# One core, linear attention and a gated FFN: half units in pairs, 12 gated units, one more q transposed by TensorE, single stores, another order

## The chip, the core and the metric

The kernel runs on one core of a Trainium2 chip. The metric is the device time of one execution in microseconds. The five engines each take their own instructions in order: TensorE (PE, with its weight loads PEld), VectorE (DVE), ScalarE (ACT), GpSimd (POOL) and SyncE (SP), which here issues nearly all DMAs. An engine's part that issues and waits is written with a q (SPq, ACTq).

## The reference

```python
def _attn_ref(q, k, v):                      # 8 batches, 8 heads, 576 tokens, 64 wide
    q_s = np.exp(q - np.max(q, axis=-1, keepdims=True))
    q_s = q_s / (np.sum(q_s, axis=-1, keepdims=True) + 1e-09)
    k_s = np.exp(k - np.max(k, axis=2, keepdims=True))      # over the tokens
    k_s = k_s / (np.sum(k_s, axis=2, keepdims=True) + 1e-09)
    kv = np.einsum('bhsd,bhse->bhde', k_s, v)
    return np.einsum('bhsd,bhde->bhse', q_s, kv)

def _moe_ref(x, w_in, w_out, beta):          # x: 4608 x 512, w_in 512 x 2048, w_out 2048 x 512
    h = x @ w_in
    g = h * (1.0 / (1.0 + np.exp(-beta * h)))
    return g @ w_out
```

x is the attention's output with the heads side by side. All inputs and the output are float32.

## The kernel before

**Layout.** A batch's 576 tokens are read as 64 x 9: token p*9 + i lies on partition p, with two heads' 64 partitions on top of each other, so that four tiles j hold eight heads. i = 0 to 7 are the main part (512 tokens), i = 8 the tail (64 tokens). There are nine chunks of 512 tokens: one per batch, and one (number 7, `TAILS`) with the tails of all eight; the chunk behind it, number 8, is batch 7.

**Attention of a batch b.** VectorE takes the maxima of q (`q_max`, L360) and POOL subtracts them (`q_sub`, L376); ScalarE takes the exponential (`q_exp`, L383); VectorE sums and inverts (`q_sum` L406, `q_rcp` L412 and L413); POOL scales and casts to bf16 (`q_norm`, L421). Then q must be transposed. Batch 0 does that on TensorE (`q_tr`, L442, with evictions by `q_tr_ev`); batches 1 to 7 do it with a DMA that SyncE issues (`q_tr_dma`, L428). For k, VectorE takes maxima over the tokens (`k_max` L462, `k_red` L473, `k_small` L494 and L497, `k_rep` L515), POOL subtracts (`k_sub`, L525), ScalarE takes the exponential (`k_exp`, L532). `kv_mm` (L556) makes kv in two PSUM banks, 72 small matmuls; `kv_norm` (L575 to L578, VectorE) makes kvn from it; `x_mm` (L606) multiplies kvn with the transposed q into four banks, and `x_ev` casts each of them into xT, the FFN's input, with tokens in the order (i, p). `xt_mm` (L645) and `xt_ev` do the tail.

**FFN.** A unit n is one chunk and one block of 128 of the 2048 inner columns, so there are 9 x 16 = 144 units. `st1` (L758) makes h in one PSUM bank with 4 matmuls of 512 columns; `tanh` (L774, ScalarE) and `gate` (L787, VectorE, out = (tanh + 1) * h) make g, in one of NG = 8 buffers; `st2` (L825, and L817 for the last quarter of the last chunk) adds g's product into four banks `acc`, one per 128 tokens, with 4 matmuls. At the end of a chunk `o_ev` copies the banks into osb, and `store` (L854) issues two DMAs for each 128 tokens, as each half holds the rows of another i. The first four units (`LEAD`) go in halves of 256 tokens: a bank holds one unit, and each half has a tanh and a gate of its own.

**Banks.** Four PSUM banks (`ring`) go round among h, kv, x and tails (`take`): the next taker gets the bank that was taken longest ago and is free by then.

**The order** is written out by hand: `ORDER` names every step once (h_5 is the first stage of unit 5, th_5 and g_5 its tanh and gate, o_5 its second stage, ld_ a load, st_ a store, qT_ a DMA transpose), with the engine behind = where it can be chosen. Each engine gets its instructions in this order; the semaphores between engines follow from the data. So a load or store that must wait holds up all that stands behind it on SyncE, and a maximum whose load is late holds up the gates behind it on VectorE. In the built program each DMA also waits for the landing of the one eight before it. Before the first FFN matmul TensorE runs dummy matmuls (`fill`, L349). The weights come in eight loads of two halves; each half is cast to bf16 on POOL or ScalarE.

Of the kernel before, what the change touches and what calls it, by code (L numbers as in the profile page):

```python
# [17 lines left out]
ld_q0_0, consts, qmax_0_2_0, qmax_0_0_0, qsub_0_0_0=pool, qmax_0_1_0, qexp_0_0_0, qsub_0_2_0=pool, ld_q0_1,  # L18
qmax_0_0_j3, qmax_0_2_1, ld_k0_1, qmax_0_1_1, qmax_0_0_j2, qexp_0_0_j3, qsum_0_0_0, ld_beta, kmax_0_1, ld_k0_0,
qsub_0_1_1=pool, qsub_0_1_0=pool, kmax_0_0, qsub_0_2_1=pool, fill_0, fill_1, fill_12, fill_13, beta_tr, fill_8,  # L20
fill_10, qexp_0_0_j2, fill_2, fill_9, qexp_0_1_0, qrcp_0_0, kred_0, fill_11, qexp_0_1_1, qexp_0_2_0, ld_v0_1,
vcast_0_j3=pool, kswap_0, ld_v0_0, qsum_0_1_0, qsum_0_2_0, qnorm_0_0_0=pool, qtr_0_0_0, ksmall_0, qsum_0_1_1,
krep_0_0, krep_0_1, ksub_0_2=dve, ksub_0_0=dve, qnorm_0_0_1=pool, vcast_0_j0=act, qexp_0_2_1, qsum_0_2_1,
vcast_0_j1=act, ksub_0_3=pool, vcast_0_j2=pool, fill_15, ld_q1_1, qrcp_0_1, fill_4, fill_14, qtrev_0_0_0=act,
kexp_0_2, qtr_0_0_1, kexp_0_3, kexp_0_0, ld_w0_1, ld_w0_0, ld_k1_1, ksub_0_1=dve, kexp_0_1, fill_16, kv_0_1, beta_ev,
kv_0_0, qmax_1_3, cast_w0_0_1=act, qmax_1_2, ld_w1_0, ld_w2_0, qnorm_0_1_0=pool, qnorm_0_1_1=pool, qtr_0_1_0,
qtr_0_1_1, fill_3, kvn_0, cast_w0_1_1=act, qtrev_0_1_0=act, qtrev_0_0_1=dve, x_0_0_1, x_0_0_0, xev_0_0_0=act,
cast_w0_1_0=pool, fill_5, qrcp_0_2, qtrev_0_1_1=dve, cast_w0_0_0=pool, xev_0_0_1=dve, qsub_1_1=pool, fill_7, x_0_1_1,
x_0_1_0, h_0_0_0, h_0_0_1, h_2_0_0, xev_0_1_0=act, qnorm_0_2_1=pool, kmax_1_3, xev_0_1_1=dve, th_0_0, g_0_0, h_3_0_0,
fill_6, cast_w2_0=pool, h_3_0_1, qexp_1_3, qnorm_0_2_0=pool, th_3_0, ld_w2_1, qexp_1_2, h_1_0_0, h_1_0_1, h_0_1_0,  # L30
h_2_0_1, cast_w1_0=pool, cast_w2_1=pool, ld_w1_1, h_2_1_0, h_2_1_1, h_0_1_1, h_3_1_0, th_1_0, h_1_1_0, ld_k1_0,
h_1_1_1, h_3_1_1, ld_w4_1, qsum_1_3, ld_w4_0, kmax_1_2, th_0_1, qsum_1_2, g_0_1, ld_w3_0, th_2_0, th_1_1, th_2_1,
ld_q1_0, ld_w3_1, o_0_0, th_3_1, g_3_0, g_2_0, g_2_1, qrcp_1_1, o_0_1, h_5, cast_w1_1=pool, qnorm_1_1=pool, ld_w6_1,
cast_w4_1=pool, g_3_1, g_1_0, g_1_1, kmax_1_1, kmax_1_0, kred_1, th_5, ksmall_1, h_4, g_5, o_1_0, th_4, h_6, th_6,
krep_1, g_4, o_1_1, h_7, o_2_0, o_2_1, o_3_0, cast_w4_0=pool, g_6, cast_w3_0=act, h_8, th_7, th_8, ld_w5_0, qmax_1_0,
qmax_1_1, ld_w6_0, ksub_1_0=pool, o_3_1, h_9, th_9, qsub_1_0=pool, h_11, o_4, cast_w3_1=act, o_5, o_6, g_7, o_7, g_8,
ld_w5_1, ld_q2_1, h_10, cast_w5_0=pool, cast_w6_1=act, th_11, ld_v1_1, qexp_1_1, ld_w7_0, o_8, g_11, qexp_1_0, g_9,
qsum_1_0, qsum_1_1, ksub_1_1=pool, cast_w6_0=act, th_10, qtrt_0, qtrtev_0_0=act, h_12, cast_w5_1=act, kexp_1_3, o_9,
h_14, kexp_1_0, th_12, qtrtev_0_1=dve, qrcp_1_0, kexp_1_1, th_14, g_10, qmax_2_2, qmax_2_3, qnorm_1_0=pool, h_15,
h_13, ld_v1_0, ld_w7_1, cast_w7_0=act, g_14, g_12, th_13, g_13, vcast_1_1=pool, qsub_2_1=pool, kexp_1_2, th_15, g_15,  # L40
vcast_1_0=pool, o_10, o_11, qexp_2_3, qexp_2_2, o_12, o_13, cast_w7_1=pool, qsum_2_3, kv_1_0, kv_1_1, o_14, qT_1,
kvn_1, qsum_2_2, x_1_1, x_1_0, xev_1_2=act, xev_1_0=dve, xev_1_3=dve, xev_1_1=act, qrcp_2_1, ld_q2_0, o_15, h_17_0,
qmax_2_0, ld_v2_1, ld_k2_1, ld_k2_0, h_17_1, qmax_2_1, oev_0_3=act, th_17, ld_q3_0, h_16_0, g_17, h_16_1, th_16,
g_16, ld_v2_0, ld_k3_0, h_18, th_18, oev_0_2=act, g_18, kmax_2_3, h_24, oev_0_0=act, h_21, th_21, kmax_2_0,
qnorm_2_1=pool, kmax_2_1, h_20, oev_0_1=act, qsub_2_0=pool, g_21, h_19, o_16, o_17, h_22, th_20, kmax_2_2, o_18,
qmax_3_0, g_20, th_19, g_19, ld_v3_0, qexp_2_1, th_24, th_22, kred_2, ksmall_2, vcast_2_1=pool, h_23, g_22, krep_2,
ld_k3_1, th_23, qmax_3_1, g_23, qexp_2_0, kmax_3_2, ld_q3_1, h_26, st_0_1, o_19, o_20, h_25, vcast_2_0=act, g_24,
qsum_2_1, kmax_3_3, ld_q4_0, o_21, h_27, qsum_2_0, th_26, o_22, vcast_3_0=pool, ksub_2_1=pool, kexp_2_2, th_25, g_26,
g_25, kexp_2_3, ksub_2_0=pool, th_27, o_23, g_27, ld_v3_1, o_24, o_25, xt_0, kexp_2_0, kexp_2_1, kv_2_0, kv_2_1,
xtev_0_0=act, xtev_0_1=act, h_30, h_28, kmax_3_0, qrcp_2_0, qnorm_2_0=pool, kmax_3_1, qsub_3_0=pool, qmax_3_2, kvn_2,  # L50
qmax_3_3, kred_3, th_30, th_28, g_28, st_0_3, qsub_3_1=pool, vcast_3_1=pool, h_29, o_26, ld_q4_1, h_31, st_0_0,
ld_k4_1, st_0_2, th_29, ksmall_3, g_29, g_30, qT_2, th_31, o_27, o_28, o_29, g_31, krep_3, x_2_1, xev_2_3=act, x_2_0,
xev_2_0=dve, xev_2_2=dve, qexp_3_1, ld_k4_0, o_30, o_31, xev_2_1=act, kmax_4_1, qexp_3_2, h_34, oev_1_2=act, th_34,
ksub_3_0=pool, ksub_3_1=pool, h_32, oev_1_1=dve, th_32, oev_1_3=act, qmax_4_1, h_33, oev_1_0=act, th_33, qexp_3_3,
g_34, g_32, ld_v4_1, h_35, qsum_3_1, ld_v4_0, th_35, st_1_1, ld_q5_1, h_37, h_36, qmax_4_3, kexp_3_3, g_33, th_36,
qmax_4_2, th_37, g_35, qmax_4_0, o_32, g_37, qsum_3_2, g_36, vcast_4_1=pool, vcast_4_0=pool, h_38, kexp_3_0, o_33,
th_38, h_39, qsum_3_3, qsub_4_1=pool, qexp_3_0, kexp_3_1, qsub_4_0=pool, th_39, g_39, qrcp_3_1, h_42, o_34, qsum_3_0,
kexp_3_2, th_42, g_38, h_40, th_40, g_40, qnorm_3_1=pool, o_35, ld_k5_1, o_36, o_37, st_1_2, ld_q5_0, g_42, xt_1,
xtev_1_0=act, qrcp_3_0, xtev_1_1=dve, kmax_4_0, kmax_4_2, kv_3_0, kv_3_1, xt_2, kvn_3, xtev_2_1=dve, qmax_5_2,
kmax_4_3, kred_4, ksmall_4, xtev_2_0=act, o_38, o_39, o_40, h_43, qnorm_3_0=pool, h_41, qT_3, qexp_4_2, qexp_4_3,  # L60
th_43, g_43, th_41, g_41, kmax_5_2, krep_4, h_46, ld_k5_0, qexp_4_0, th_46, qexp_4_1, h_44, h_45, th_45, th_44, g_46,
o_41, o_42, st_1_3, o_43, g_44, x_3_0, st_1_0, g_45, x_3_1, ksub_4_1=pool, qsum_4_3, qmax_5_3, ksub_4_0=pool, o_44,
xev_3_2=act, h_47, th_47, xev_3_0=act, kmax_5_0, o_45, xev_3_1=dve, o_46, qsum_4_2, qsum_4_0, kmax_5_3, xev_3_3=act,
h_48, th_48, h_50, qsum_4_1, g_47, h_51, qsub_5_1=pool, h_49, g_48, th_50, qmax_5_0, g_50, ld_v6_1, th_51, h_52,
o_47, th_49, g_49, oev_2_1=dve, h_53, h_54, qrcp_4_1, g_51, oev_2_2=act, th_52, g_52, qnorm_4_1=pool, h_57, kmax_5_1,
kexp_4_2, oev_2_0=act, oev_2_3=dve, h_56, st_2_3, qexp_5_3, th_54, qexp_5_2, qrcp_4_0, o_48, o_49, ld_q7_1, st_2_0,
g_54, kred_5, qsum_5_3, o_50, qnorm_4_0=pool, th_53, qmax_5_1, o_51, h_60, qsub_5_0=pool, g_53, th_57, g_57, h_55,
th_56, g_56, th_55, o_52, th_60, g_60, h_59, ksmall_5, kexp_4_0, th_59, krep_5, g_59, ld_v5_1, h_62, ld_v5_0, qT_4,
qexp_5_0, kexp_4_3, st_2_1, st_2_2, o_53, h_63, th_63, th_62, kexp_4_1, o_54, h_58, ld_q6_1, g_55, g_62, o_55,
qsum_5_0, ksub_5_1=pool, kexp_5_3, th_58, o_56, o_57, g_58, qsum_5_2, qexp_5_1, g_63, ksub_5_0=pool, o_58, h_61,  # L70
kv_4_0, kv_4_1, ld_q7_0, ld_q6_0, qmax_6_3, qmax_6_2, kexp_5_2, th_61, kvn_4, o_59, g_61, o_60, qsum_5_1, qrcp_5_1,
qrcp_5_0, x_4_1, x_4_0, xev_4_1=dve, o_61, xev_4_0=act, o_62, kexp_5_1, o_63, xev_4_3=dve, oev_3_1=dve,
qsub_6_1=pool, xev_4_2=act, h_64, th_64, g_64, h_66, th_66, h_65, g_66, ld_k6_1, ld_v6_0, h_69, h_67, oev_3_0=dve,
th_65, g_65, th_69, qmax_6_0, g_69, h_68, oev_3_2=act, th_67, h_72, th_68, oev_3_3=act, qnorm_5_0=pool,
qnorm_5_1=pool, vcast_6_1=pool, g_68, g_67, vcast_5_1=pool, kmax_6_3, ld_v7_1, th_72, kexp_5_0, kmax_6_2, ld_k7_1,
st_3_3, ld_k6_0, qmax_7_3, h_75, ld_k7_0, o_64, h_70, th_70, h_71, g_70, th_71, o_65, qmax_7_2, o_66, o_67, g_72,
# [39 lines left out]
def kernel(  # L116
# [29 lines left out]

# [779 lines left out]
```

## Time and profile before

| | us |
|---|---|
| median of 3 runs (lowest, highest) | 293.31 (292.52, 293.66) |
| the profiled execution | 294.5 |
| its span, from first to last instruction | 292.7 |
| PE, DVE, ACT, POOL busy | 276.3, 199.6, 170.4, 130.7 |
| DMA queue of SyncE and ScalarE (q1), share of 16 engines | 57.3% |
| 140 tanhs of 512 columns, mean | 0.687 |
| 140 gates of 512 columns, mean | 0.680 |
| casts of xT, ScalarE and VectorE, mean | 0.587, 0.678 |
| 70 half stores of 128 KB, issue to landing, median | 2.4 |

The page gives busy times and 40 slices of the span with tenths of busy time; times in a timeline count from the span's start. "[3.84 <-DMA qf...]" behind a line is the idle time of the engine before it, and what ended it. PEclk is the clock granted to TensorE, in tenths of full speed.

### The profile page before, as it was taken

How to read it: one execution, taken by the hardware profiler on the slowest of the kernel's cores; microseconds unless marked ns; L12 is line 12 of the kernel's file. 1: busy time of each engine (PE TensorE's matmuls, PEld its weight loads, DVE VectorE, ACT ScalarE, POOL GpSimd, SP SyncE). 2: the span in 40 equal slices, each digit the busy share in tenths (PEclk: the TensorE clock that was granted, in tenths of full speed). 3: DMA queues.
4: the chain of work that ended last, by engine and by line, in shares of the span. 5: the costliest groups of instructions: out<-in, count | busy, mean ns of one | idle time of the engine just before them, and what ended most of it. 6: DMA issues, size and time to landing. Idle time of an engine off the chain costs nothing.

```text
span 292.7 us, 5174 instructions
## 1 busy us (share of the span) xinstructions
PE 276.3 (94%) x1922; PEld 128.7 (44%) x1951; DVE 199.6 (68%) x414; ACT 170.4 (58%) x297; POOL 130.7 (45%) x92
## 2 busy tenths in 40 slices
PE   7589999999999999996999999999999999999993
PEld 2255444444444544443344444444444444445551
DVE  3898867899799989774598968654754362456250
ACT  3687797866596656681375456845754255245342
POOL 5698986737987292661816473742002000000000
PEclk9889999999999999999799999999999999999999
DMA  7999999999954860699466908200410450005006
GB/s 247 392 391 385 386 380 208 394 383 357 231 185 155 209 215 0 176 229 304 164 204 226 179 23 164 61 2 0 111 34 2 81 125 21 0 1 129 17 0 143
DMA packets 39736, 50.60 MB, mean 173 GB/s; under 512 B 18576, under 2 KB 18848, under 8 KB 39712
## 3 DMA queue, kind: packets, MB, share of 16 engines
q1 hardware_dynamic: 39552, 50.15, 57.3%
q8 instruction: 15, 0.25, 0.3%
q10 hardware_dynamic: 160, 0.13, 0.2%
q14 instruction: 9, 0.07, 0.1%
HBM read 36.71 MB, written 9.44 MB: 158 GB/s over the span
## 4 chain that ended last, share of the span: by engine, by line
PE 73%; DMA 9%; DVE 6%; ACT 4%; issue 2%; SPq 2%; POOL 1%; POOLq 1%; ACTq 0%; DVEq 0%
PE hT L758 36%; PE acc L825 33%; DMA kf<-in_k_dram 6%; ACT th L774 2%; DMA qT<-qn 2%; DVE g L787 2%; DMA qf<-in_q_dram 1%; PE hT L606 1%; PE hT L556 1%; SPq L854 1%; ACT ek L532 1%; POOL kf L525 1%; DVE qs L406 1%; DMA out_dram<-osb 1%; POOLq L921 1%
## 5 line engine op out<-in xcount | busy, mean ns | idle before, releaser
L774 ACT ACTIVATE th<-hT,beta_c 128x512 bf16<-128x512 f32 (+1 forms) x148 | 97.1, 675 | 73.8 <-PE hT L758 59.4
L787 DVE SCALAR_TENSOR_TENSOR g<-th,hT 128x512 bf16<-128x512 bf16 (+1 forms) x148 | 94.8, 665 | 59.0 <-ACT th L774 56.7
L825 PE MATMUL acc<-w_out_b,g 128*128 128x512 bf16 x543 | 132.6, 381 | 1.3 <-issue 0.8
L758 PE MATMUL hT<-xT,w_in_b 128*128 128x512 bf16 (+1 forms) x519 | 119.1, 372 | 1.2 <-DVE g L787 0.7
L758 PEld LDWEIGHTS <-w_in_b 128*128 128x128 bf16 x592 | 57.6, 98 | 66.5 <-issue 1.2
L825 PEld LDWEIGHTS <-g 128*128 128x128 bf16 x560 | 53.8, 98 | 65.1 <-issue 4.3
L421 POOL TENSOR_TENSOR qn<-eq,qz 128x1152 bf16<-128x1152 bf16 (+2 forms) x20 | 34.6, 1738 | 50.8 <-DVE qz L413 35.0
L525 POOL TENSOR_TENSOR kf<-kf,kmb 128x1152 f32<-128x1152 f32 (+1 forms) x15 | 37.9, 2544 | 15.8 <-DVE kmb L515 10.0
L376 POOL TENSOR_TENSOR qf<-qf,qm 128x1152 f32<-128x1152 f32 (+2 forms) x19 | 33.3, 1768 | 20.1 <-DVE qm L360 13.2
L360 DVE TENSOR_REDUCE qm<-qf 128x9 f32<-128x576 f32 (+3 forms) x35 | 23.2, 688 | 8.3 <-DMA qf<-in_q_dram 8.2
L462 DVE TRANSPOSE_TENSOR_REDUCE km<-kf 128x18 f32<-128x576 f32 (+1 forms) x30 | 23.7, 803 | 1.8 <-DMA kf<-in_k_dram 1.6
L383 ACT ACTIVATE eq<-qf 128x576 bf16<-128x576 f32 (+2 forms) x33 | 20.9, 653 | 5.2 <-POOL qf L376 4.2
L406 DVE TENSOR_REDUCE qs<-eq 128x9 f32<-128x576 bf16 (+2 forms) x33 | 23.1, 706 | 0.1
L532 ACT ACTIVATE ek<-kf 128x576 bf16<-128x576 f32 x32 | 21.3, 684 | 2.4 <-POOL kf L525 2.3
L226 ACT CAST xT<-hT 128x512 bf16<-128x512 f32 x15 | 8.3, 587 | 18.7 <-PE hT L606 18.7
L228 POOL CAST va<-vf 128x1152 bf16<-128x1152 f32 (+1 forms) x14 | 14.9, 1080 | 7.7 <-DMA vf<-in_v_dram 7.7
L226 ACT COPY osb<-acc 128x512 f32<-128x512 f32 x23 | 13.0, 585 | 4.8 <-PE acc L825 2.2
L758 PE MATMUL hT<-xTt,w_in_b 128*128 128x512 bf16 x62 | 14.7, 379 | 0.1
L228 DVE COPY osb<-acc 128x512 f32<-128x512 f32 (+1 forms) x13 | 8.3, 659 | 7.0 <-PE acc L825 6.1
L349 PE MATMUL hT<-g,warm 128*128 128x512 bf16 x25 | 9.7, 512 | 1.6 <-POOL g L234 1.5
L228 DVE CAST xT<-hT 128x512 bf16<-128x512 f32 x13 | 8.3, 678 | 3.1 <-PE hT L606 3.0
L606 PE MATMUL hT<-qT,kvn 64*64 64x512 bf16 x56 | 5.4, 418 | 2.9 <-DVE kvn L578 2.5
(62 smaller groups left out, 106.5 us busy)
## 6 DMA issues: line engine op xcount, KB each, us to landing
qf<-in_q_dram SPq DMA_DIRECT2D x16, 576.0 KB, 5.0
kf<-in_k_dram SPq DMA_DIRECT2D x16, 576.0 KB, 7.3
vf<-in_v_dram SPq DMA_DIRECT2D x16, 576.0 KB, 7.6
out_dram<-osb SPq DMA_DIRECT2D x70, 128.0 KB, 2.4
wst<-in_moe_w_in_dram SPq DMA_DIRECT2D x8, 512.0 KB, 11.3
wst<-in_moe_w_out_dram SPq DMA_DIRECT2D x8, 512.0 KB, 11.1
out_dram<-osb SPq DMA_DIRECT2D x2, 64.0 KB, 2.0
out_dram<-osb ACTq DMA_DIRECT2D x2, 64.0 KB, 2.4
```

What stands on the lines that cost most here:

```text
L228: eng.tensor_copy(dst, src)
L360: dve.tensor_reduce(qm[:, j : j + n, i0:i1], qf[b % 2][:, j : j + n, i0:i1], axis=AX.X, op=ALU.max, negate=negate,)
L376: eng.tensor_tensor(x, x, m, ALU.subtract)
L406: dve.tensor_reduce(qs[:, i0:i1, j : j + n, 0:1], eq[:, i0:i1, j : j + n, :], axis=AX.X, op=ALU.add)
L421: eng.tensor_tensor(qn[b % 2][:, i0:i1, j : j + n, :], eq[:, i0:i1, j : j + n, :], z, ALU.mult)
L462: dve.tensor_reduce(km[:, j : j + n].rearrange("p j i e -> p (j i e)"), kf[b % 2][:, j : j + n].rearrange("p j i (e c) -> p (j i e) c", c=32),
L525: eng.tensor_tensor(x, x, m, ALU.subtract)
L532: act.activation(ek[b % 2][:, j : j + n], kf[b % 2][:, j : j + n], ACTF.Exp)
L758: pe.matmul(place[("h", n)][:, cols(h)], w_in_b[:, kt, u * P : (u + 1) * P], x[:, kt, cols(h)], start=(kt == 0), stop=(kt == KT - 1),)
L774: act.activation(th[n % 3][:, cols(h)], place[("h", n)][:, cols(h)], ACTF.Tanh, scale=beta_c[:, u : u + 1])
L787: dve.scalar_tensor_tensor(out=g[n % NG][:, cols(h)], in0=th[n % 3][:, cols(h)], scalar=1.0, in1=place[("h", n)][:, cols(h)], op0=ALU.add, ...
L825: pe.matmul(acc[t][:], g[n % NG][:, t * P : (t + 1) * P], w_out_b[:, u, :], start=(u == 0), stop=(u == NJ - 1),)
```

## The change

- **Half units in pairs.** For the first four units a bank now holds the same 256 tokens of two units (0 and 1, or 2 and 3). Each has its tanh; one gate does both, four gates of 512 columns for eight of 256.
- **12 gated units.** NG = 12; the buffers lie in pairs, so that one gate can write two.
- **Batch 1's q** is transposed by TensorE, 16 transposes and 2 for the tail, with four evictions, in place of the DMA. Batches 2 to 7 keep the DMA.
- **One store per 128 rows.** xT and xTt now hold tokens in an order in which a block of 128 alternates between two values of i; the evictions of x write every second element. A block's rows then lie in pairs next to each other in the output, and one DMA does them. The last quarter goes in two halves of 256 columns, one from SyncE, one from ScalarE.
- **A new order** of all steps, with other engines for some casts and evictions. Each engine's instructions stand in a new sequence.
- A path that would subtract k's maxima on TensorE is there, and not in use (`KPE` is empty); a constant for it, `minus`, is still made on POOL.

```diff
-    NG = 8
+    KPE = range(0)
+    NG = 12
...
-    g = [sbt(f"g{i}", [P, 512], BF16) for i in range(NG)]
+    gq = [sbt(f"g{i}", [P, 2, 512], BF16) for i in range(NG // 2)]
+    g = [gq[i // 2][:, i % 2] for i in range(NG)]
...
+        pool.memset(minus[:], 0.0)
+        pool.affine_select(
+            out=minus[:],
...
+    def mixed(x):
+        return x.rearrange("p (t c i) -> p t i c", i=2, c=64)
...
-        cast(eng, xT[b % 2][:, j, :], place[("x", b, j)])
+        cast(eng, mixed(xT[b % 2][:, j, :]), place[("x", b, j)].rearrange("p (t i c) -> p t i c", i=2, c=64))
...
-        op(f"qT {b}", lambda b=b: q_tr_dma(b))
+        if b > 1:
+            op(f"qT {b}", lambda b=b: q_tr_dma(b))
+            continue
+        for J in range(2):
+            op(f"qtr {b} {J}", lambda b=b, J=J: q_tr(b, J, 0, NM))
+            op(f"qtrev {b} {J}", lambda e, b=b, J=J: q_tr_ev(b, J, 0, NM, e), "act")
+            op(f"qtrtev {b} {J}", lambda e, b=b, J=J: q_tr_ev(b, J, NM, 1, e), "act")
+        op(f"qtrt {b}", lambda b=b: [q_tr(b, J, NM, 1) for J in range(2)])
...
+    def bank(n, h):
+        key = ("h", n) if h is None else ("hp", n // 2, h)
+        if key not in place:
+            take(key)
+        if h is None:
+            return place[key]
+        return place[key][:, 256 * (n % 2) : 256 * (n % 2) + 256]
...
+            out = gq[n // 2][:, :, cols(h)]
+            of = th[turn(n, h) % 3][:].rearrange("p (m t) -> p m t", m=2)
+            src = place[("hp", n // 2, h)].rearrange("p (m t) -> p m t", m=2)
+        dve.scalar_tensor_tensor(out=out, in0=of, scalar=1.0, in1=src, op0=ALU.add, op1=ALU.mult)
...
-    def store(c, t, engs=(sp, sp), x=None):
+    def store(c, t, eng=sp, x=None):
...
+            rows = out[b * S : (b + 1) * S, :].rearrange("(p i) f -> p i f", i=NI)[:, 2 * t : 2 * t + 2]
+        eng.dma_start(rows[:, :, f], osb[:, t, f])
```

The places in the new order that the prediction speaks of:

```python
..., kv_2_0, kv_2_1, xt_0, xtev_0_0=act, ld_k4_0, o_21, xtev_0_1=dve, qnorm_2_0=pool, qsub_3_0=pool, o_22, ...
o_23, o_24, kvn_2, o_25, o_26, qsub_3_1=pool, g_31, qexp_3_2, kmax_3_2, g_30, kred_3, qsum_3_2, qT_2, x_2_0, ...
st_1_3, ksub_4_0=pool, qT_3, st_1_2, ..., g_46, ld_q6_1, qmax_6_2, ld_k5_1, kmax_5_2, ld_q6_0, ...
st_2_3, ..., ld_q7_1, ld_v6_0, vcast_6_0=act, qT_4, ..., st_2_2, ..., st_2_0, ld_q7_0, ...
x_5_1, x_5_0, xev_5_2=act, xev_5_0=dve, o_75, xev_5_1=act, xev_5_3=dve, h_81, ...
```

More of the change, by code (lines that the diff above doesn't have):

```diff
@@ L342, in fill @@
         done.add(key)
[L343 removed]
+        r = g[NG - 1]
         if part is not None:
@@ L520, in k_sub @@
     def k_sub(b, j, n, eng):
-        uses("kmb", *[(x, eng if b == 0 else None) for x in pairs_of(b, j, n)])
+        uses("kmb", *[(x, dve if b == 0 and eng is dve else None) for x in pairs_of(b, j, n)])
         made("ksub", *pairs_of(b, j, n))
@@ L525, in k_sub, with kn_bank, k_in, k_minus @@
         eng.tensor_tensor(x, x, m, ALU.subtract)
+    def kn_bank():
+        if "kn" not in place:
+            take("kn")
+        return place["kn"][:, 0 : len(KPE) * D]
+    def k_in(j):
+        if j is None:
+            rhs = kf[0][:, 0 : len(KPE), NM, :]
+        else:
+            rhs = kf[0][:, j, 0:NM, :]
+        w = kn_bank() if j is None else acc[j][:]
+        made("kin", j)
+        pe.matmul(w, ident_f[:], rhs, start=True, stop=False)
+    def k_minus(j):
+        uses("kin", j)
+        made("kminus", j)
+        if j is not None:
+            made("ksub", (0, j))
+        if j is None:
+            uses("kmb", *[((0, x), None) for x in KPE])
+            rhs = kmb[:, 0 : len(KPE)]
+        else:
+            uses("kmb", ((0, j), None))
+            rhs = kmb[:, j].unsqueeze(1).to_broadcast((P, NM, D))
+        pe.matmul(kn_bank() if j is None else acc[j][:], minus[:], rhs, start=False, stop=True)
+    def k_exp_pe(j):
+        uses("kminus", j)
+        if j is None:
+            made("kexpn", 0)
+            done.add("kn")
+            act.activation(
+                ek[0][:, 0 : len(KPE), NM, :], kn_bank().rearrange("p (j d) -> p j d", d=D), ACTF.Exp
+            )
+            return
+        made("kexp", (0, j))
+        act.activation(ek[0][:, j, 0:NM], acc[j][:].rearrange("p (i d) -> p i d", d=D), ACTF.Exp)
     def k_exp(b, j, n):
@@ L547, in kv_mm @@
         uses("va", *pairs_of(b, 2 * J, 2))
+        if b == 0 and KPE:
+            uses("kexpn", 0)
         made("kv", (b, J))
@@ L754, in st1 @@
                 uses("xT", *[(c - (c > TAILS), kt, a) for a in halves(h)])
-        if ("h", n) not in place:
-            take(("h", n))
+        if h is not None and n % 2 and ks[0] == 0:
+            uses("st1", (n - 1, h))
+        if ks[0]:
+            uses("begun", (n, h))
+        made("begun", (n, h))
+        w = bank(n, h)
         for kt in ks:
             pe.matmul(
-                place[("h", n)][:, cols(h)],
+                w,
                 w_in_b[:, kt, u * P : (u + 1) * P],
```

297 lines of the change are left out of this document (158 added, 139 removed).

## The prediction

> **What bounds the kernel now.** I read the page first, its busy shares and its 40 slices, then TensorE's busy time by stretches of the span, then the timeline around the two stretches that are not full, last the order of the built programs.
>
> ```profile
> PE 276.3 (94%) x1922; PEld 128.7 (44%) x1951; DVE 199.6 (68%) x414; ACT 170.4 (58%) x297; POOL 130.7 (45%) x92
> PE   7589999999999999996999999999999999999993
> PEclk9889999999999999999799999999999999999999
> ```
>
> TensorE (PE) is full from slice 4 on, but for slice 19 and the last one; in slice 20 its granted clock falls too. So the time is: when the first FFN matmul starts, plus TensorE's work, plus what TensorE loses, plus what follows its last matmul. The stretches (time, PE, PEld, DVE, ACT, POOL, clock, DMA share, GB/s) say how much it loses where:
>
> ```profile
> 20.96:27.15 6.19, 5.51 (x44) 3.96 (x42) 5.16 (x11) 4.91 (x11) 5.08 (x7) 1.00 1.05 385
> 27.15:49.94 22.79, 22.68 (x174) 10.34 (x175) 17.40 (x41) 18.14 (x27) 19.73 (x12) 1.00 1.01 328
> 49.94:78.83 28.89, 28.71 (x214) 13.05 (x220) 26.54 (x59) 18.77 (x31) 18.96 (x11) 1.00 1.00 342
> 78.83:105.50 26.67, 26.41 (x214) 12.17 (x218) 23.81 (x51) 19.36 (x34) 18.37 (x10) 1.00 0.70 210
> 133.75:140.70 6.95, 3.88 (x89) 1.69 (x90) 3.86 (x12) 0.69 (x1) 2.12 (x1) 0.89 0.98 349
> ```
>
> TensorE's own work: the chain has 20 matmuls of 512 columns in 4.32 us, 0.216 each. The two FFN stages are 1152 such: 248.8 us. Batches 1 to 7 add the kv matmuls (72 in about 0.65), the x matmuls (8 in 0.56), and 8 sets for the tails (0.16): 4.6 + 3.9 + 1.3, and 0.3 of small things. Sum 258.9 us. From the first FFN matmul (20.96) to the end of the last (288.04) are 267.1, so 8.2 are lost: 1.0 before 27.15 (5.2 of work in 6.19), 1.05 in 27 to 134, 4.9 between 133.75 and 144.22 (where 5.5 of work stands), 1.1 afterwards. The 4.9 has this story:
>
> ```profile
> 122.61 7.40 SPq L428 DMA_TRANSPOSE qT<-qn  x1
> 130.05 2.52 SPq L854 DMA_DIRECT2D out_dram<-osb  x4
> 132.61 1.64 SPq L259 DMA_DIRECT2D qf<-in_q_dram  x3
> ...
> 136.74 1.41 DVE L360 TENSOR_REDUCE qm<-qf 128x9 f32<-128x576 f32 x2 [3.84 <-DMA qf<-in_q_dram]
> 138.53 0.49 DVE L578 TENSOR_TENSOR kvn<-hT,kz 128x128 bf16<-128x128 f32 x2
> 138.88 0.40 PE L606 MATMUL hT<-qT,kvn 64*64 64x512 bf16 x1 [2.52 <-DVE kvn L578]
> 140.66 3.72 PE L825 MATMUL acc<-w_out_b,g 128*128 128x512 bf16 x12
> ```
>
> SyncE's queue (SPq) stands 7.40 us in the transpose of batch 4's q (five of the other six took 2.7 to 3.1, the first 3.44); two v loads had been issued 1.2 us before it. Behind it four half stores take 2.52, and only then are batch 6's q loads issued. VectorE, which takes its work in order, waits 3.84 for them with kvn of batch 4 queued behind, and TensorE waits for kvn. Then 12 matmuls take 3.72 where 12 x 0.216 + 0.17 = 2.76 would do. And the end:
>
> ```profile
> 285.28 4.96 SPq L854 DMA_DIRECT2D out_dram<-osb  x8
> 287.00 1.04 PE L817 MATMUL hT<-w_out_b,g 128*128 128x256 bf16 x8
> 288.07 0.37 ACT L226 COPY osb<-hT 128x256 f32<-128x256 f32 x1 [0.29 <-DMA out_dram<-osb]
> 288.47 0.48 ACTq L854 DMA_DIRECT2D out_dram<-osb  x1
> ```
>
> Eight stores stand in SPq until 290.24, 1.77 us after ScalarE's queue has begun the last half. The last SPq issue began at 289.69.
>
> **The change, part by part.**
>
> *TensorE's work.* Batch 1's q costs 18 more transposes. The row of batch 0's says 8 in 0.75 with one alone at 0.27, so 0.07 each: +1.2. One dummy matmul fewer stands behind the first FFN matmul (-0.2). **+0.9 us**, all on the path. They also need evictions on ScalarE and VectorE (about 1.7 and 0.7, from 0.58 and 0.405 per 512 columns and 0.265 per tail), which have gaps there (ACT 18.14 of 22.79). What leaves is one DMA transpose: 3.44 of SPq, and the fall from about 386 to 186 GB/s in 45 to 50.
>
> *Start.* On VectorE kmax of the first half now stands behind a q sum (0.68) and a reciprocal pair (0.4); a small sum leaves the way. I get the last k subtraction at 17.2 instead of 16.57, kvn at 19.4 instead of 19.36 (two q maxima of 0.7 now stand ahead of it, in time that was idle), the first FFN matmul at 21.0 instead of 20.96. Zero, give or take 0.7. The w loads keep seven half loads ahead of them. The constant that nothing reads costs POOL a memset and a select, 0.38 + 0.31 by the rows of swap, inside its 2.21 of idle.
>
> *Half units in pairs.* Eight gates of 0.41 become four of about 0.66: VectorE saves 0.6. A gate now waits for two tanhs, and what is queued behind it (the next gates, batch 1's sums) waits too. In rows: 32 half matmuls end at 24.5; the first pair's second tanh ends at 23.6, its gate at 24.3, so unit 6 starts on time; unit 4 needs the gate at 25.7 and waits 0.4. After that four whole units are ahead of the first second-stage matmul, and its weights (cast on POOL by 27.1) are there at 28.3. So 0.4 is lost where 1.0 was: **-0.6**.
>
> *12 gated units.* Nothing is added; gates wait later for their buffers. Counted from the first FFN matmul with the rows' durations, the TensorE work queued ahead of a unit's use exceeds the VectorE work queued ahead of its gate by 4.4 us or more; before, by 2.6 or more. That hides tanh and gate (0.69 + 0.68).
>
> *Stores.* 36 issues fewer of 0.55. The tail: after the last matmul 0.4 for the eviction, then ScalarE's issue of 128 KB, which landed in 2.4 in the row of that size: last landing 2.8 after the matmul. Before it was 289.69 + 2.0 (median of the 64 KB pieces) = 291.7, 3.65 after. The 1.0 from landing to the span's end stays. **-0.8**.
>
> *The new order, 134 to 144.* In the new program batch 4's transpose is followed on SPq by two single stores and q of batch 7; batch 6's q and k are issued one batch earlier, behind batch 3's transpose. Counting VectorE's and POOL's rows up to there (qnorm ready near 94, x of batch 3 due at 105) they land 5 us or more ahead of their maxima. So the 4.9 goes: **-4.9**. What is late next: x of batch 2, whose transpose I get issued at 68.7 and landed at 73.4 (4.7) against a place at 75.5; three loads stand just ahead of it, as two did in the bad case (9.5 to landing).
>
> *Strided writes.* The x evictions write every second 2-byte element. No row of before does that. Below: no gain, since the count of elements is the same. Above: twice the part beyond start-up, about +0.53 on 0.59 and 0.68. I take none: casting to 2 bytes costs what the 4-byte copy does (587 against 585 ns on ScalarE, 678 against 679 on VectorE), so writing isn't what sets it. The Trainium skill's page SBUF — State Buffer (section Door 1: The DMA port swizzle, its note on 16-byte lines) lets bf16 be strided up to 8 elements apart without loss; by that the term is 0 too, and no run here shows it yet.
>
> *Shorter covers.* Between x of batch 5 and the first FFN matmul that needs it stands 0.86 of other matmuls; before, 2.6. Two VectorE evictions end about 1.35 after x: **+0.5**.
>
> Sum: +0.9 - 0.6 - 0.8 - 4.9 + 0.5 = -4.9. From the profiled execution (span 292.7, time 294.5): 289.6. The shown runs have their median 1.2 below it, 293.31; the forecast is **288.5 us**.
>
> **Rivals.**
>
> *VectorE becomes the bound early.* Between x of batch 0 and x of batch 3 its queue gets 3 more q maxima, 4 sums, 2 reciprocal pairs and less of gates and evictions: about +3.1 us. It was busy 72.9 of 84.5 there. For: 92% busy from 50 to 79. Against: that excess of TensorE work is 12 to 20 us for units 12 to 24, where it was 4.5 to 12. If its 11.6 of waits all stay, the stretch takes 72.9 + 3.1 + 11.6 = 87.6 where TensorE needs 83.5 and some 1.4 of losses: x of batch 3 comes 2.8 late, 291.3.
>
> *A new stall of the old kind.* Batch 2's transpose held behind three loads, with x directly behind it: 9.5 - 4.7 - 2.1 of slack gives 2.7, plus a slow clock afterwards (about 1.0, as in 140.66) and what follows: up to 4.9 again, 293.4. The Trainium skill's page TensorE: Matmul & The Clock Gate (Part 1: The HAM clock gate) ties the slow clock to an idle window of about 3.4 us; by it a stall of 2.7 could stay without the 1.0, and the rival would give 291.2. The trace speaks against that: TensorE stood idle from 136.35 to 138.88 only, and the granted clock was 0.89 over the stretch.
>
> *Strided writes cost double: slower.* Four x evictions per batch, two on each engine, so the last comes 1.06 later; the covers (0.86 to 2.6 of matmuls) are mostly used already, so 8 batches lose up to 8.5: 297.0. It decides from about 1.1 us for an eviction. For: no row shows it. Against: the equal rows above.
>
> *The stores don't gain.* If the merged store lands as late as the pair did, 289.3.
>
> **How the numbers follow.** Forecast 0.62, stores without gain 0.06, VectorE 0.15, a new stall 0.11, strided writes 0.06. Half a per cent (1.5 us) is about what a measurement here can tell from none: faster below 291.8. The forecast, the stores and 0.10 of VectorE's lie there: 0.78. Same: 0.05 of VectorE's and 0.08 of the stall: 0.13. Slower: 0.06 and 0.03 of the stall: 0.09. The range takes the start (0.7) and all of the small losses (2) away below: 285.8; above it reaches the new stall: 293.9.
>
> **What would show it.** First FFN matmul near 21; slice 19 full and the clock at 9 throughout; SPq done before ScalarE's last issue, under 4 us after the last matmul; x evictions at 0.59 and 0.68. Wrong: an eviction above 0.8, a wait for a q load or for a transpose of over 2 us, or VectorE at 95% and TensorE waiting for gates.

## The result, and the profile after

The kernel after takes 291.22 us (median of 20 runs, 289.91 to 293.72), the kernel before 293.38 beside it (20 runs, 291.35 to 295.60): ratio 0.9934, 95% interval 0.9911 to 0.9958. So it is faster by 0.7%, 2.2 us, where 4.9 were forecast. In two series of the experiments below, each with its own runs of before, it stood 3.3 and 3.5 below before (ratios 0.9883, interval 0.9840 to 0.9927, and 0.9885, 0.9852 to 0.9919): after was 291.05 and 291.00 there, before 294.37 and 294.48.

The page of after, profiled in an execution of 289.91 with a span of 287.9, the quickest of its 20:

```profile
PE 277.1 (96%) x1969; PEld 128.6 (45%) x1969; DVE 202.1 (70%) x413; ACT 175.0 (61%) x302; POOL 127.8 (44%) x90
PE   7769999999999999999999999999999999999994
PEclk9999999999999999999999999999999999999999
```

The hole in slice 19 and the fall of the clock behind it are gone. By stretches, from each batch's x to the next (us, then busy time and count of PE, PEld, DVE, ACT, POOL, then clock, DMA share, GB/s):

```profile
19.69:46.20 26.51, 25.67 (x214) 13.43 (x213) 21.34 (x48) 21.10 (x36) 22.55 (x18) 1.00 1.05 387
...
75.40:105.67 30.27, 29.57 (x228) 13.47 (x227) 26.15 (x60) 22.27 (x40) 24.94 (x12) 1.00 0.79 232
...
164.96:193.46 28.50, 28.50 (x214) 12.73 (x213) 16.45 (x32) 13.77 (x22) 8.11 (x5) 1.00 0.35 107
```

TensorE is idle for 0.84 in the first stretch, 0.70 in the one from 75.40 and 0.41 in the one from 105.67, and in no other. VectorE is busy 28.09 of the 29.20 from 46.20 to 75.40 and holds nobody up there: that rival is out. This one execution is close to the forecast for the profiled pair (289.6), but it is not a typical one: the median is 1.3 above it. What after waits for is in two views. First the waits of ScalarE (us in total, times, longest):

```profile
ACT osb L230 <- DMA out_dram<-osb: 3.0, 2, 1.6
```

Two output evictions wait for a store to land, 1.58 and 1.45, since they write the same place of osb as the chunk before. TensorE stands idle 0.70 behind the first and 0.34 behind the second (the expectation of a_osb2 below says 0.69 for the second). In before the same row is shorter:

```profile
ACT osb L226 <- DMA out_dram<-osb: 0.8, 2, 0.5
```

And the start of after, timeline of 18 to 30:

```profile
18.91 0.73 ACT L230 CAST xT<-acc 128x512 bf16<-128x512 f32 x1
...
19.69 1.14 PE L861 MATMUL hT<-xT,w_in_b 128*128 128x256 bf16 x9 [0.48 <-ACT xT L230]
20.72 0.73 DVE L232 CAST xT<-acc 128x512 bf16<-128x512 f32 x1 [0.73 <-PE hT L861]
20.76 0.73 ACT L230 CAST xT<-acc 128x512 bf16<-128x512 f32 x1 [1.12 <-PE hT L861]
...
21.55 6.20 PE L861 MATMUL hT<-xT,w_in_b 128*128 128x256 bf16 x39 [0.71 <-ACT xT L230]
```

The first FFN matmul is 1.3 earlier than before's 20.96, but after nine of them TensorE waits 0.71 for the second half of x, whose two evictions begin only when matmuls of the first half have ended. A strided eviction takes 0.73 where 0.585 and 0.672 stood before.

### The profile page after: what moved, and what is told of

Same layout as the page of the kernel before. It is cut to its first block, busy times and chain, and to the rows that moved or that the text cites. A ratio compares the mean times of both kernels' runs of the same rounds, so it can differ in the third digit from the quotient of the medians.

```text
span 287.9 us, 5187 instructions
## 1 busy us (share of the span) xinstructions
PE 277.1 (96%) x1969; PEld 128.6 (45%) x1969; DVE 202.1 (70%) x413; ACT 175.0 (61%) x302; POOL 127.8 (44%) x90
## 4 chain that ended last, share of the span: by engine, by line
PE 74%; DVE 9%; DMA 7%; ACT 4%; POOL 2%; issue 2%; SPq 1%; ACTq 0%; DVEq 0%
PE acc L927 36%; PE hT L861 34%; DMA out_dram<-osb 6%; DVE g L896 2%; POOL kf L543 2%; DVE km L478 2%; ACT th L879 2%; DVE qm L374 1%; PE hT L617 1%; DMA qf<-in_q_dram 1%; ACT xT L230 1%; DVE qs L420 1%; PE hT L667 1%; SPq L273 1%; DVE kf L543 1%
## 5 line engine op out<-in xcount | busy, mean ns | idle before, releaser
L879 ACT ACTIVATE th<-hT,beta_c 128x512 bf16<-128x512 f32 (+1 forms) x148 | 95.2, 677 | 72.1 <-PE hT L861 53.5
L896 DVE SCALAR_TENSOR_TENSOR g<-th,hT 128x512 bf16<-128x512 bf16 x144 | 94.4, 678 | 58.8 <-ACT th L879 49.2
L230 ACT CAST xT<-hT 128x512 bf16<-128x512 f32 x18 | 12.3, 741 | 14.7 <-PE hT L667 14.7
L591 ACT ACTIVATE ek<-kf 128x576 bf16<-128x576 f32 x32 | 20.6, 685 | 0.3 <-POOL kf L543 0.2
L232 DVE COPY osb<-acc 128x512 f32<-128x512 f32 x18 | 11.9, 681 | 4.0 <-PE acc L927 3.9
L230 ACT COPY osb<-acc 128x512 f32<-128x512 f32 (+1 forms) x18 | 10.0, 576 | 7.2 <-PE acc L927 3.1
L232 POOL CAST va<-vf 128x1152 bf16<-128x1152 f32 x8 | 9.2, 1148 | 2.0 <-PE hT L617 2.0
L230 ACT CAST va<-vf 128x1152 bf16<-128x1152 f32 (+1 forms) x10 | 9.4, 961 | 0.5 <-DMA vf<-in_v_dram 0.5
L232 DVE CAST xT<-hT 128x512 bf16<-128x512 f32 x10 | 6.7, 727 | 4.1 <-PE hT L667 4.0
```

The lines of the kernel that those rows point to most:

```text
L230: act.copy(dst, src)
L232: eng.tensor_copy(dst, src)
L879: act.activation(th[turn(n, h) % 3][:, c], bank(n, h), ACTF.Tanh, scale=beta_c[:, u : u + 1])
L896: dve.scalar_tensor_tensor(out=out, in0=of, scalar=1.0, in1=src, op0=ALU.add, op1=ALU.mult)
```

## The experiments

Times are medians in us; the ratio is to the kernel before on the same chip, estimated from all runs, so it is not exactly the quotient of the two medians. Kernels whose name begins with b are made from before, with a from after.

**1. The old stall alone.**

```diff
-... g_59, ld_v5_1, h_62, ld_v5_0, qT_4,
+... g_59, ld_q6_1, ld_q6_0, ld_v5_1, h_62, ld_v5_0, qT_4,
```

> The kernel before, with batch 6's two q loads issued ahead of batch 5's v loads and batch 4's transpose on SyncE's queue, and nothing else. It prices the stall of 133 to 144 us in typical executions. Theory A (the prediction's -4.9 is right, and the kernel after gives some of it back elsewhere): the stall goes and the time falls by 4 to 5 us, to about 288.5 to 289.5. Theory B (the profiled execution of before, 294.5, was an untypical one, and the stall is mostly smaller): it falls by 2 to 3 us, to 290.5 to 291.5. Theory C (a v load or the transpose, now later, becomes late in its place): it falls by less than 1 us, and the trace shows DVE or PE waiting for qT or v of batch 4 or 5.

Measured: 289.65 against 294.37, ratio 0.9833 (0.9793 to 0.9873): -4.7. Theory A holds. The page has no hole any more:

```profile
PE   6689999999999999999999999999999999999993
```

So two loads issued ahead of two v loads and a transpose gave more than the whole change did. The prediction's largest term was right on this chip, and the kernel after must lose elsewhere. The six runs of b_q6early spread over 1.1 us (289.12 to 290.25) where before's eleven spread over 3.9, so most of before's spread seems to lie in that stall.

> The kernel before, unchanged, for a second profiled execution. Theory (the stall is a fixed part of it): between 133 and 145 us TensorE again loses 4.5 to 5 us. Rival (the first profile had a long one): 2 to 3.5 us there, and a time near 293.0.

Measured: 294.86, and the same chain, with waits of 4.58 and 3.25 where the first profile had 3.84 and 2.52 (timeline of 120 to 146):

```profile
136.78 1.41 DVE L360 TENSOR_REDUCE qm<-qf 128x9 f32<-128x576 f32 x2 [4.58 <-DMA qf<-in_q_dram]
...
138.92 0.40 PE L606 MATMUL hT<-qT,kvn 64*64 64x512 bf16 x1 [3.25 <-DVE kvn L578]
```

From the kv matmuls of batch 4 to the first-stage matmuls behind its x, TensorE takes 11.34 here, 10.47 in the first profile and 5.74 in b_q6early. So the stall cost 5.6 and 4.7 in these two executions: it comes each time, as the theory has it, but its size differs.

**2. Evictions that don't wait for the last chunk's store.**

```diff
-        if c:
-            uses("store", (c - 1, t))
+        if c > 1:
+            uses("store", (c - 2, t))
...
-        cast(eng, osb[:, t, :], acc[t][:])
+        cast(eng, osb[c % 2][:, t, :], acc[t][:])
```

> The kernel after, with two output blocks in turn, so that an eviction to osb waits for the store of two chunks earlier and not for that of the last one. The merged stores land behind queued loads (6.9 and 9.1 us after issue where the median is 2.9), and ScalarE's evictions wait 1.58 and 1.45 us for them, with tanhs queued behind; TensorE loses 0.70 and 0.69 there in the profiled execution. Theory (these waits are part of what the typical execution loses): 1.2 to 2.5 us less than the kernel after, 288.7 to 290.0, and no eviction waits for a store. Rival (the TensorE work queued ahead absorbs them, or the next wait takes their place): within 0.5 us of the kernel after, 291.2.

Measured: 288.23, ratio 0.9791 (0.9750 to 0.9832), 2.8 below the kernel after on that chip: a little over the theory's upper end. The kernel after itself, profiled again in an execution of 292.6, shows why:

> The kernel after, unchanged, for a second profiled execution beside the same runs of before. Theory (the first profile was a lucky execution): its own time is near 291.2, and the stretches between the x matmuls lose 1 to 2 us more than the 4.6 of the first, at evictions that wait for a store's landing or at x that waits for a transpose. Rival (the difference is spread evenly, as by a clock a little lower): the same waits with the same numbers, and all stretches longer by the same share.

Measured: 291.05 median. Its profile loses more than the theory's 1 to 2 us, nearly all of it at one place. SyncE's queue there (72 to 92):

```profile
81.00 0.47 SPq L273 DMA_DIRECT2D qf<-in_q_dram  x1
81.51 1.19 SPq L954 DMA_DIRECT2D out_dram<-osb  x2
```

This load and two more, issued from 79.05 on, 576 KB each, stand ahead of the two stores, which land 8.2 after their issue (median of all stores in the page of after: 3.5). Then, in the timeline of 86 to 97:

```profile
89.75 0.59 ACT L230 COPY osb<-acc 128x512 f32<-128x512 f32 x1 [3.31 <-DMA out_dram<-osb]
...
90.96 0.69 DVE L896 SCALAR_TENSOR_TENSOR g<-th,hT 128x512 bf16<-128x512 bf16 x1 [3.15 <-ACT th L879]
...
91.70 1.25 PE L861 MATMUL hT<-xT,w_in_b 128*128 128x512 bf16 x4 [2.43 <-DVE g L896]
...
92.74 3.39 PE L927 MATMUL acc<-w_out_b,g 128*128 128x512 bf16 x8
```

ScalarE stands 3.31 for the landing with a tanh queued behind, VectorE waits for the tanh, TensorE for the gate, 2.43; and then its matmuls take 0.42 each instead of 0.216 (the eight at 92.74). The stretch behind the wait, with its clock in the third column from the right:

```profile
91.70:96.13 4.43, 4.43 (x13) 1.66 (x13) 4.23 (x12) 4.43 (x9) 3.63 (x2) 0.61 0.01 2
```

13 matmuls take 4.43 where 13 x 0.216 = 2.8 would do, so this one late store cost 2.4 + 1.6 = 4.0. In the first profile the same eviction waited 1.58 and TensorE 0.70. From x of batch 2 to x of batch 4 it takes 61.11 here, 58.43 in the first profile and 56.83 in a_osb2, so the waits for landings cost 4.3 and 1.6 in these two executions. With two output blocks the same part of the program, 75.40 to 105.60, has TensorE busy throughout (27.77 in again_after, 29.50 in the first profile):

```profile
75.40:105.60 30.20, 30.20 (x234) 13.74 (x233) 26.85 (x62) 22.92 (x41) 25.90 (x13) 1.00 0.81 231
```

> The kernel after, unchanged, on the same chip as the next three, to take differences from. Theory (how long it waits for the stores' landings differs between executions): its times spread over 2 us or more, and this profile loses 1 to 4 us at g behind an eviction that waits for a store. Rival: the same waits as in the first profile, 1.4 in all.

> Two output blocks in turn, once more beside the kernel after. Theory (the waits for landings cost 2.8): 2.3 to 3.2 below the kernel after, and a spread under 1 us but for single executions. Rival (half of the 2.8 was the other chip or the hour): 1 to 2 below it.

Measured side by side on one chip: after 291.00 (290.20 to 292.80; this profile's wait is 1.6 of TensorE), two blocks 288.61 (288.19 to 288.77), ratio 0.9791 (0.9765 to 0.9818). The landings cost **2.4** by these medians (2.8 on the other chip), and with them goes most of after's spread.

**3. Is it the single store, or the stores' place?** x plain and two half stores per block, everything else as in after:

```diff
-        eng.dma_start(rows[:, :, f], osb[:, t, f])
+        for s in range(2):
...
+            engs[s].dma_start(rows[:, f], osb[64 * s : 64 * s + 64, t, f])
```

> The kernel after with the part 'one store per block of 128 rows' undone: x written without a stride, and two stores of 64 rows each per block, as before; order, half units, 12 gates and batch 1's q stay. Theory (the waits for landings come from the new places of the stores in SyncE's queue, not from their size): evictions still wait 1 us or more for a store's landing; the unstrided x gives 1.0 back, the tail costs 0.9 and 36 issues more some tenths: 290.5 to 292. Rival (a store of 256 KB is what lands late): no eviction waits above 0.8 us, and the time falls to 288 to 289.5.

Measured: 291.96, ratio 0.9959 (0.9929 to 0.9989). Its waits for landings are longer yet:

```profile
ACT osb L230 <- DMA out_dram<-osb: 5.2, 2, 2.7
```

So the theory holds: two half stores in the places of the new order wait as well, and a single store isn't needed for it. Before's longest such wait was 0.5.

**4. Strided writes.** (Both kernels store a block's rows in another order, as said in the expectations.)

```diff
-        cast(eng, mixed(xT[b % 2][:, j, :]), place[("x", b, j)].rearrange("p (t i c) -> p t i c", i=2, c=64))
+        cast(eng, xT[b % 2][:, j, :], place[("x", b, j)])
```

> The kernel after, with the x evictions written without a stride (each token's column where the kernel before put it) and everything else as it is; the rows of one block of 128 so stand in another order in the output, which changes no instruction's size. It prices the strided writes alone. If the 741 ns of a strided ScalarE eviction against 587 come from the stride, the rows go back to 587 and 678, and since two evictions stand one behind the other on an engine ahead of the first FFN matmul of most batches, 8 times 0.05 to 0.2 us come back: 0.4 to 1.5 us less than the kernel after. Rival (the rows have another cause, or other TensorE work covers them): rows unchanged, or time within 0.3 us of the kernel after.

> Two output blocks in turn and x written without a stride, each block's rows so stored in another order in the output. No eviction waits for a store, so the price of the strided writes stands alone. Theory (0.15 us per eviction where two stand one behind the other, at the start and between batches): 0.5 to 1.2 below two output blocks with strided writes, the first FFN matmuls without the 0.71 stall at 21. Rival (TensorE work covers them everywhere but at the start): 0.3 to 0.7 below, all of it before 27 us.

Measured: a_plain 290.00 (after 291.05 beside it), ratio 0.9841, with landing waits of its own; a_osb2_plain 287.11 (two blocks with the stride: 288.61), ratio 0.9752 (0.9724 to 0.9781). The strided writes cost 1.05 by the first pair, whose landing waits differ, and **1.5** by the second, above both expectations. The groups by shape, mean ns behind the busy time, first in after, then in a_plain:

```profile
L230 ACT CAST xT<-hT 128x512 bf16<-128x512 f32 x18 | 12.3, 741 | 14.7 <-PE hT L667 14.7
...
L232 DVE CAST xT<-hT 128x512 bf16<-128x512 f32 x10 | 6.7, 727 | 4.1 <-PE hT L667 4.0
```

```profile
L230 ACT CAST xT<-hT 128x512 bf16<-128x512 f32 x18 | 9.8, 591 | 14.9 <-PE hT L667 14.9
...
L232 DVE CAST xT<-hT 128x512 bf16<-128x512 f32 x10 | 6.4, 686 | 4.2 <-PE hT L667 4.0
```

In these rows the strided write is also cut into eight runs of 64 elements, and the plain one is not. The tail's evictions tell the two apart, as both kernels write them in two runs of 64 and only the stride differs (after, then a_plain):

```profile
L230 ACT CAST xTt<-hT 128x128 bf16<-128x128 f32 x7 | 2.0, 305 | 6.2 <-PE hT L709 6.2
```

```profile
L230 ACT CAST xTt<-hT 128x128 bf16<-128x128 f32 x7 | 1.8, 265 | 6.2 <-PE hT L711 6.2
```

VectorE's are 295 and 282. Four times these differences is 160 and 52, about what the whole rows lost (150 and 41), so the stride explains it.

The start of a_osb2_plain, against the timeline of after above:

```profile
19.13 1.07 ACT L230 CAST xT<-acc 128x512 bf16<-128x512 f32 x2
19.77 7.27 PE L863 MATMUL hT<-xT,w_in_b 128*128 128x256 bf16 x48 [0.34 <-ACT xT L230]
```

No stall, and ScalarE's two evictions follow each other. From the first FFN matmul to x of batch 1 it takes 25.64 where after and a_osb2_2 take 26.51, 0.87 more. Beside that, the profile of a_osb2_2 loses 0.14 between x of batch 0 and the first FFN matmul and 0.24 between x of batches 4 and 6, and nowhere else more than 0.02: 1.25 in all. (The rest of the difference between the two profiles stands ahead of batch 0's x, where nothing is written with a stride.) So more than half of the price is the wait of 0.71. One run moves the place of the two late evictions alone:

```diff
-... xev_0_0_1=dve, h_0_0_0, ..., xev_0_1_1=act, ..., xev_0_1_0=dve, ...
+... xev_0_0_1=dve, xev_0_1_1=act, xev_0_1_0=dve, h_0_0_0, ...
```

> Two output blocks in turn, with the two evictions of the second half of batch 0's x placed ahead of the first FFN matmuls in the program instead of behind eight of them. In the kernel after these two start when the eighth FFN matmul ends (20.72), although the matmuls read other columns; without the stride they start at once. Theory (the program's tracking takes the strided write of one half to overlap the reads of the other, and adds a wait): placed ahead, the same mistake makes the first FFN matmuls wait for all four evictions: they begin 0.6 to 0.9 us later, near 20.6, without the stall of 0.71, and the time stays within 0.4 us of 288.4. Rival (the wait is a real one, on a PSUM bank or on the engines' turn, and only the place counts): the first FFN matmul stays near 19.9 and the stall goes: 0.6 to 0.8 us less, 287.7.

Measured: 288.14 on another chip, ratio 0.9767 (0.9729 to 0.9805); theory and rival are 0.7 apart, so the time does not decide, and the profile must. Its start:

```profile
19.69 1.32 ACT L230 CAST xT<-acc 128x512 bf16<-128x512 f32 x2
20.47 0.27 PE L861 MATMUL hT<-xT,w_in_b 128*128 128x256 bf16 x1 [0.48 <-ACT xT L230]
21.18 3.01 PE L861 MATMUL hT<-xT,w_in_b 128*128 128x256 bf16 x26 [0.44 <-DVE qz L426]
```

All four now run through, and one matmul starts as early after them as before (0.78 behind the first eviction's start); the next waits until VectorE's second eviction has ended at 21.12 (19.79 + 1.33), though it reads none of its columns. So the theory held but for that first matmul: with the stride, whichever side stands second in the program waits for the other; without it, in the late place, nobody does (the early place was not run without it). That the program's dependency tracking takes the strided region to overlap the other half is the reading that fits; the tracking itself was not looked into.

**5. Keeping the single store without the stride.**

```diff
-            rows = out[b * S : (b + 1) * S, :].rearrange("(p i) f -> p i f", i=NI)[:, 2 * t : 2 * t + 2]
+            rows = out[b * S : (b + 1) * S, :].rearrange("(p i) f -> i p f", i=NI)[2 * t : 2 * t + 2]
```

a_best has this store with x plain and two output blocks; b_merge and b_q6merge have it in before, whose x is plain.

> The kernel after with both of its suspected losses taken away: two output blocks in turn, and x written without a stride; the store still takes a block of 128 rows in one issue, but goes through the rows of the output in the order of the partitions (two runs of 64 rows, 9 rows apart each), so that the output is as it should be. Theory (the two losses are separate: 2.8 for the stores' landings, 1.05 for the strided writes): 3.9 us below the kernel after, ratio to before 0.976, about 287.2. Rival (the strided rows are covered by TensorE work once no eviction waits for a store): as with two output blocks alone, ratio 0.979, 288.2. Second rival (the rows that no longer lie side by side in DRAM make the store slower): above 288.5, and the tail after the last matmul longer than 3.7.

> The kernel before with one store per block of 128 rows (x unstrided, the store's rows in the order of the partitions), and nothing else. The prediction's term for the stores, -0.8 at the end. Theory (the term is right, and the waits for landings come from the new places of the stores in SyncE's queue): 0.5 to 1.0 us less, the last landing about 1 us earlier after the last matmul, no ScalarE wait on a store above 0.8 us. Rival (one store of 256 KB in place of two of 128 KB is what lands late behind loads): waits of over 1 us of evictions for a store's landing appear, and the time is the same or longer by up to 2 us.

> The kernel before with batch 6's two q loads issued earlier and with one store per block: the two parts of the sum that can be had without the new order. Theory (both terms add): 4.7 + 0.8 = 5.5 us below before, ratio 0.981, about 288.9 where before is 294.4; so all of the gain of the kernel after and more is in these two. Rival (with fewer issues SyncE's queue runs ahead and another load or transpose is late): no less than 289.7, ratio 0.984.

Measured: 329.56, 351.59 and 342.57, ratios 1.120, 1.195 and 1.165. All three theories missed. Of the rivals, a_best's second has the sign, a slower store and a longer tail (22 us where it said over 3.7), but it named another reason and no such size; b_q6merge's is met in its number alone. No term can be priced by these three. The tail of b_merge tells why: its last matmul ends at 328.8, and 22 us pass until the span's end, with nothing but stores (same columns as above; DMA share before the last):

```profile
334.00:340.00 6.00, 0.00 (x0) 0.00 (x0) 0.00 (x0) 0.00 (x0) 0.00 (x0) 0.50 0.13 50
```

A share of 0.13 is what two of 16 DMA engines give (2/16 = 0.125), which would be 25 GB/s each; after's tail has 0.52 and 184 GB/s:

```profile
284.20:287.90 3.70, 0.00 (x0) 0.00 (x0) 0.00 (x0) 0.35 (x1) 0.00 (x0) 0.92 0.52 184
```

The pattern's outermost dimension is 2 (two values of i) where after's is 64. The Trainium skill's page DMA: Bandwidth & Descriptors (section Rules for kernel authors) says that an outermost dimension of fewer than 16 confines a transfer to at most that many engines; this trace agrees, by its 0.13. So here the stride in x is the price of a fast single store: without it, the store took this slow pattern. Other patterns for a plain x were not tried.

**6. Single store only where it is on the path** (a_mix has two output blocks, b_mix the loads of section 1).

```diff
+        if b < B - 1:
+            cast(eng, xT[b % 2][:, j, :], place[("x", b, j)])
+            return
...
+        if c == NCH - 1:
+            rows = out[b * S : (b + 1) * S, :].rearrange("(p i) f -> p i f", i=NI)[:, 2 * t : 2 * t + 2]
+            eng.dma_start(rows[:, :, f], o[:, t, f])
+            return
+        for s in range(2):
...
+            eng.dma_start(rows, o[64 * s : 64 * s + 64, t, :])
```

> The kernel before with batch 6's two q loads issued earlier, and with the strided write and the single store for the last chunk alone. The two terms of the sum that can be had without the new order. Theory: 4.7 + 0.8 = 5.5 us below before, ratio 0.981, 288.8, the last landing 3.8 after the last matmul. Rival (the single store does nothing at the end): as with the q loads alone, 0.983 to 0.984, 289.6.

> The kernel after with two output blocks in turn, and the strided write and the single store kept for the last chunk (batch 7) alone, where the end of the kernel hangs on them; all other x are written without a stride and stored in two halves. Theory (the strided writes cost 1 us, mostly at the start and between batches, and the single store pays only at the end): about 1 us below two output blocks alone, ratio to before 0.976, 287.2. Rival (the extra store issues on SyncE's queue hold loads or transposes back, or the strided rows are covered): 0.979 or above, 288.2 or more.

> Two output blocks, strided writes and single stores for the last chunk alone, once more, on the same chip as two output blocks with and without strided writes everywhere. Theory (34 store issues more on SyncE's queue cost nothing beside loads): as x without a stride everywhere, within 0.3 us. Rival (the issues hold loads or transposes back): 0.4 to 1 us above that.

Measured: b_mix 288.61, ratio 0.9841 (0.9803 to 0.9879). Its chip's before is 0.9 lower than that of b_q6early, so that the ratios say no gain and the times 1.0; the profiles settle it for the end: 3.63 from the last matmul to the span's end against 4.68 in b_q6early. a_mix 287.64, ratio 0.9811: the time speaks for the theory, the ratio for the rival. On one chip with the others a_mix_2 has 287.51 (ratio 0.9760, 0.9733 to 0.9788) against 288.61 with the stride everywhere and 287.11 without. So the stride is worth giving up everywhere but in the last chunk. The issues more on SyncE's queue, 32 by the page where the expectation says 34, stand with 0.4 between theory and rival, inside the spread of the runs. Apart from the kernel that stores rows in another order it is the fastest here, 3.5 below the kernel after on that chip and 2.4% below before.

**7. Batch 1's q by DMA again**, with two output blocks:

```diff
-        if b > 1:
+        if b > 0:
             op(f"qT {b}", lambda b=b: q_tr_dma(b))
...
-... ld_v1_1, ..., qtrev_1_1=dve, ...
+... qT_1, ld_v1_1, ...
```

> The kernel after with two output blocks in turn and with batch 1's q transposed by a DMA, as before, ahead of batch 1's second v load on SyncE's queue. Theory (18 transposes of TensorE cost 1.2 us, and the DMA transpose holds SyncE's queue for 3.4 us, from which loads and x of batch 1 come late): TensorE's work is 1.2 less, x of batch 1 later than 43.7, time within 1 us of two output blocks alone, 287.5 to 289. Rival (the transpose lands in time): 1.2 us less, 287.0. Second rival (it lands behind the queued loads, 9 us after issue): TensorE waits 3 us or more for x of batch 1, 291 or more.

Measured: 289.74, ratio 0.9878 (0.9843 to 0.9914), 1.1 to 1.5 above two output blocks on other chips (0.9791 twice). x of batch 1 is no later (46.48 against 46.41 in a_osb2), but the transpose holds SyncE's queue for 4.56 from 34.04, and behind it stands a weight load whose cast ends late. TensorE's waits behind it:

```profile
53.00 1.02 PE L983 MATMUL acc<-w_out_b,g 128*128 128x512 bf16 x4 [0.60 <-ACT w_out_b L286]
54.30 1.02 PE L917 MATMUL hT<-xT,w_in_b 128*128 128x512 bf16 x4 [0.28 <-DVE g L952]
```

The time lies above the theory's range and below the second rival's. Only this one place of the transpose was tried.

## Why the prediction was wrong

The direction was right and the range held the time; the gain was less than half of the forecast. By its terms (us; measured on one chip or within profiles, as said above):

| step | forecast | measured | from |
|---|---|---|---|
| the stall of 134 to 144 goes | -4.9 | -4.7 | b_q6early against before; smaller on another chip, see below |
| TensorE's work | +0.9 | +0.8 | twice 0.45 from the first of eight transposes to the matmul behind them in a_osb2, 0.11 for two of a tail, 0.2 for the dummy matmul |
| first FFN matmul | 0 | -1.2 | 19.69 to 19.88 in three profiles of after, 20.41 to 21.75 in six with the start of before |
| half units in pairs | -0.6 | -0.7 | TensorE's idle time up to x of batch 1: 0.13 beside the 0.71 stall, 0.79 before |
| stores at the end | -0.8 | -0.9 to -1.0 | 3.7 against 4.7; b_mix 3.63, b_q6early 4.68 |
| shorter cover at batch 5 | +0.5 | +0.1 | first FFN matmul 1.53 after x of batch 5, where x and four matmuls take 1.42 |
| strided writes | 0 | **+1.0 to +1.5** | a_plain, a_osb2_plain |
| stores that land behind loads | not in the sum | **+2.4** | after_2 against a_osb2_2 |

With 1.25 for the strided writes they sum to -3.0, beside the -3.3 and -3.5 of the experiments. Each is good to some tenths. Two steps failed, and a third was too large for a typical execution.

*"Stores. 36 issues fewer of 0.55. The tail ..."* The new place of the stores was followed only to the end of the kernel. In the middle each output eviction waits for the landing of the store one chunk earlier, and a tanh stands behind it on ScalarE. The prediction's own last quoted ScalarE row had such a wait, 0.29 for out_dram, and the new order has `ld_q5_1, ld_v3_0, ld_q5_0, st_0_2, st_0_0` on SyncE's queue, the loads and stores of 79 to 83 above. The prediction did count that delay for the transpose of batch 2 (9.5 behind loads) and for no store. It is a stall of the old kind, as the second rival feared, with a store in the transpose's place: 2.4 us by the medians, 1.6 and 4.3 in two executions.

*"Strided writes. Below: no gain ... I take none."* The reason given was that the cast to 2 bytes took as long as the 4-byte copy. That compares two writes without a stride and says nothing of one with it. The rows became 741 and 727 from 587 and 678. The Trainium skill's page SBUF — State Buffer (section Door 1: The DMA port swizzle, the note on 16-byte lines) gave the same zero for a stride of two; the measurement decides against it here. The rival had the right sign, with 1.06 per batch; but later covers hide the longer evictions nearly everywhere, and more than half of what is lost is one added wait at the start, which none of the prediction's steps had.

*"-4.9" and "their median 1.2 below it".* The stall was priced from a profiled execution that took 1.2 longer than the median, and then the 1.2 was taken off as well. Since before's spread seems to lie mostly in that stall, part of it was probably subtracted twice. (The sum from 293.31 is also 288.4, not 288.5.) On the chip of b_mix, where before's median was 293.49, the stall comes to 3.8 by an estimate: 4.9 below before, less 1.05 for the shorter tail. With 3.8 the terms sum to -2.1, close to the -2.2 of the 20 runs; b_q6early was not run beside those, so this stays an estimate.

The start was wrong too, in the other direction: kvn of batch 0 ended at 18.42 where 19.4 was forecast and 19.36 stood before. Which of the new places does it was not looked into. That the profiled execution came out at 289.91, near the 289.6 of the sum, is in part luck: the earlier start made up for some of the landings and strided writes, none of which the sum had, and the landing waits were short in this execution.

## What to carry to other kernels

When an order is changed, follow every DMA to whoever waits for its landing, stores too: a buffer that is written again one chunk later makes each store a dependency of the compute engine, and a second buffer (1 MB here) takes it away. A single large store is worth its price only where the end hangs on it; look at the outermost dimension of its pattern first. Price a suspected stall in the old kernel by moving the loads alone: here that edit gave -4.7 where the whole change gave -2.2 to -3.5. And take the size of a stall and the time it is subtracted from out of the same execution, or both from medians.

## What the hardware showed unexpectedly

- A store whose outermost dimension is 2 moved 50 GB/s at a DMA share of 0.13, and the kernels with it took 35 to 57 us more than before.
- Writing bf16 with a stride of two elements took ScalarE 741 ns for 128x512 instead of 591 without it, and VectorE 727 instead of 686.
- TensorE idled 2.43 in again_after and then ran at a granted clock of 0.61 over the next 4.43; after 1.56 of idle time in after_2 the clock stayed at 1.00. By the Trainium skill's page TensorE: Matmul & The Clock Gate (Part 1: The HAM clock gate) the clock falls after an idle window of about 3.4 us; here, as in before's stall (2.52), a shorter idle time was enough.
